# Spreading a routing decision over two turns, and a reordered lead-in, in an RWKV-then-router kernel

## The chip, the core and the metric

The kernel runs on one core of one Trainium2 chip. Its time is device microseconds from launch to end, the median of several runs. All arithmetic is float32. A core has five engines that run their own instruction queues: TensorE (PE, with its weight loads shown as PEld), VectorE (DVE), ScalarE (ACT), GpSimd (POOL) and SyncE (SP), which here only starts transfers. An engine executes its queue in program order; a semaphore makes it wait for another engine or a transfer.

## The reference, cut to what matters

A linear-attention recurrence over 768 steps (4 batches, 8 heads of 48) gives 3072 rows of 384. Each row is then sent to one of 8 experts, the one whose embedding is nearest in angle, and multiplied by its softmax weight.

```python
for t in range(S):                                   # S = 768
    cur = einsum('bhd,bhe->bhde', u[None] * kt, vt)
    y[:, :, t] = einsum('bhd,bhde->bhe', rt, state + cur)
    state = w[None, :, :, None] * state + einsum('bhd,bhe->bhde', kt, vt)
# x = y as rows (B*S, H*D) = (3072, 384)
logits = xn @ en.T / tau                             # xn, en: rows of norm one
expert_idx = argmax(logits, axis=1)                  # gate_w: its softmax weight
for e in range(E):                                   # E = 8, F = 1024
    h = maximum(x[mask] @ w1[e], 0.0)                # mask = expert_idx == e
    out[mask] = gate_w[mask, None] * (h @ w2[e])
```

## The kernel before

The sequence is cut into chunks of 128 steps; six chunks for each of four batches give 24 *units*. The decay `w` is clamped, its powers 1 to 128 are put into `wpow`, and two tables follow: `rpow` (powers over the middle power) scales the turned queries, and `kpow` (the reversed ones, turned) scales the keys. A *turn* of the loop `attention` has a unit in each stage: it turns the next unit's queries and keys (`rt`, `kt`), adds up its state (`st`), sums two products for the output (`y`), computes the next scores (`at`), and turns the output back to rows (`yrows`, then `X`). Between these lie the steps of the routing, a group of four units at a time: logits (`lgT`, `lg`), the choice, ranks, and lists of tokens for each expert (`take`, summed in `sums`).

After 16 of the 24 units are routed, the kernel *settles* which two experts are least loaded, so that the loading of their weights and one full tile of rows of each can start before the routing is over. Afterwards come those two early tiles, and then one `Block` per expert.

The start, cut:

```python
def build_first(k):
    ...                                              # wc is loaded by two DMAs
    ps = k.ps.tile([128, 512], F32, name="wake", tag="tp")
    for _ in range(WAKE):                            # WAKE = 3: products that warm TensorE up
        nc.tensor.matmul(ps, k.ones, wide, start=True, stop=True)
    ...                                              # 11 small memsets of Kpad and Rpad on GpSimd
    load(k, 0, nc.scalar)                            # K, R, V of unit 0; R on ScalarE's queue
    load(k, 1)
    load_consts(k)                                   # u_bc, emb, tau, wrow, all on ScalarE's queue
    build_consts(k)                                  # GpSimd: umask, states = 0, ent, iotas, ...
    for i in range(2, AHEAD - 1):
        load(k, i)
    own(k, 0)                                        # GpSimd: KU = K * u_bc * R

    nc.vector.tensor_scalar(wc, wc, W_MIN, W_MAX, ALU.max, ALU.min)
    t = pool.tile([128, NP, C], F32, name="wpow")
    ...                                              # 4 scans: powers; mid = 1 / t[:, :, 64]
    nc.vector.tensor_mul(kp, t[:, :, ::-1], over_i)
    ...                                              # TensorE turns kp into ps (kpT)
    nc.vector.tensor_mul(k.rpow, t, over_i)
    nc.vector.tensor_mul(k.Kpad[0]..., k.loaded[0][0]..., cols)   # cols = kpT
    turn_r(k, 0)                                     # rt, then RT = rt * rpow on VectorE
    k.kpow = pool.tile([128, H, D], F32, name="kpow")
    nc.vector.tensor_copy(k.kpow..., cols)
    turn_k(k, 0)                                     # kt, then KT = kt, copied by ScalarE
```

The state of a batch, whose first unit meets zeros:

```python
def carry(k, i):
    ...
    nc.vector.tensor_add(T[0:PP], T[0:PP], st[0:PP])
    nc.gpsimd.tensor_mul(T[0:PP], T[0:PP], k.wC[0:PP])
```

The loop, cut to what the change touches; `j = i - 12`, so `j == 8` is unit 20:

```python
    for i in range(-1, units):
        ...                                          # load, summed, turn_r, turn_k, scaled, own, states
        whole(choose, i - 3)
        ...
        on(own_sum, i + 1)                           # diag = sums of KU, VectorE
        if j == 7:
            load_, count = loads(k, "xp")
        if i == units - 2:
            own_rows_once(k, i + 1)                  # xd of the last unit, GpSimd
        if j == 9:
            perm = turner(k, k.by)                   # VectorE: hit, perm
            k.lists = turned_lists(k, perm, "st")    # TensorE: lists = sums x perm
            lists = taken_by_rank(k, k.lists)        # VectorE: none, take, gates
            first = [Early(k, r, *lists, w) for r, w in zip(LAST, k.weights)]   # gathers, GpSimd
            load_w2(k, number, k.weights[0][1])
        on(sums, i)                                  # y
        ...
        on(scores, i + 1)                            # at
        on(masked, i + 1, 0)
        on(rows, i)                                  # yrows, X
        on(masked, i + 1, 1)
        ...
        if j == 8:
            settle(k, load_, count)
            number = expert_number(k, LAST[0])
            load_w1(k, number, k.weights[0][0])

def settle(k, load, count):
    by = order(k, load)                              # VectorE: more, by
    nc.vector.tensor_scalar(k.settled, by, float(min(LAST)) - 1, None, ALU.max)
    expert_of(k, by)                                 # VectorE: eq, is_e, who
    k.by = by
    ...                                              # VectorE: lack, last, lack, cum
```

The last columns of an expert whose count isn't a multiple of 128 (two row tiles, three transposes each):

```python
    def rest(self):
        ...                                          # yT[:, m, :] for m = 0..2: TensorE, then a ScalarE copy
        for t, (_, _, gate, here) in list(enumerate(self.tiles))[2:]:
            ps = k.ps.tile(...)
            if n % 128:
                for m in range(NK):
                    nc.tensor.transpose(ps[0:here, m * 128 : (m + 1) * 128], yT[:, m, at], k.ident)
            ...
            nc.scalar.mul(y[0:here], ps[0:here, 0:DM], gate[0:here])
            self.put(t, y)
```

Of the kernel before, what the change touches and what calls it, by code (L numbers as in the profile page):

```python
# [47 lines left out]
def build_first(k):  # L48


    nc, pool = k.nc, k.aconst
    wc = pool.tile([128, NP], F32, name="wc")
    nc.vector.memset(wc, 1.0)
    with nc.allow_non_contiguous_dma(reason="384 words"):
        for s, q in ((0, nc.sync), (1, nc.scalar)):
            q.dma_start(out=wc[s * DP : s * DP + D, :], in_=k.w.rearrange("(p s) d -> s d p", s=2)[s])
    k.ones = k.const.tile([128, 128], F32, name="ones")
    nc.vector.memset(k.ones, 1.0)
    wide = k.work.tile([128, 512], F32, name="wide", tag="AT1")
    nc.vector.memset(wide, 1.0)  # L60
    k.ident = k.const.tile([128, 128], F32, name="ident")
    make_identity(nc, k.ident)

    ps = k.ps.tile([128, 512], F32, name="wake", tag="tp")
    for _ in range(WAKE):
        nc.tensor.matmul(ps, k.ones, wide, start=True, stop=True)
    for lst, name, count in ((k.Kpad, "Kpad", 4), (k.Rpad, "Rpad", AHEAD + 2)):
        for i in range(count):
            t = pool.tile([128, H, DP], F32, name=f"{name}{i}")
            nc.gpsimd.memset(t[:, :, D:DP], 0.0)  # L70
            lst.append(t)
    load(k, 0, nc.scalar)
    load(k, 1)
    load_consts(k)
    build_consts(k)
    for i in range(2, AHEAD - 1):
        load(k, i)
    own(k, 0)


    nc.vector.tensor_scalar(wc, wc, W_MIN, W_MAX, ALU.max, ALU.min)
    t = pool.tile([128, NP, C], F32, name="wpow")
    for p in range(NP):
        nc.vector.tensor_tensor_scan(
            t[:, p, :], wc[:, p : p + 1].to_broadcast([128, C]), k.ones, 1.0, ALU.mult, ALU.mult
        )
    mid = pool.tile([128, NP], F32, name="mid")
    nc.vector.reciprocal(mid, t[:, :, C // 2])
    over_i = mid[:, :, None].to_broadcast([128, NP, C])
    kp = k.work.tile([128, NP, C], F32, name="kp", tag="AT0")  # L90
    nc.vector.tensor_mul(kp, t[:, :, ::-1], over_i)
    ps = k.ps.tile([128, NP, 2, DP], F32, name="kpT", tag="xp")
    for p in range(NP):
        nc.tensor.transpose(ps[:, p].rearrange("q s d -> q (s d)"), kp[:, p, :], k.ident)
    k.rpow = pool.tile([128, NP, C], F32, name="rpow")
    nc.vector.tensor_mul(k.rpow, t, over_i)
    cols = ps[:, :, :, 0:D]
    nc.vector.tensor_mul(
        k.Kpad[0].rearrange("q (p s) d -> q p s d", s=2)[:, :, :, 0:D],
        k.loaded[0][0].rearrange("q (p s) d -> q p s d", s=2), cols,  # L100
    )
    turn_r(k, 0)
    k.kpow = pool.tile([128, H, D], F32, name="kpow")
    nc.vector.tensor_copy(k.kpow.rearrange("q (p s) d -> q p s d", s=2), cols)  # L104
    turn_k(k, 0)
    k.wC = t[:, :, C - 1 : C].to_broadcast([128, NP, D])


# [5 lines left out]
    return f  # L114


def load_consts(k):
    nc = k.nc
    k.u_bc = k.aconst.tile([128, H, D], F32, name="u_bc")
    nc.scalar.dma_start(  # L120
        out=k.u_bc.rearrange("p h d -> p (h d)"),
        in_=bass.AP(tensor=k.u.tensor, offset=k.u.offset, ap=[[0, 128], [1, DM]]),
    )
    k.emb_rows = k.aconst.tile([E, DM], F32, name="emb")
    nc.scalar.dma_start(out=k.emb_rows, in_=k.emb)
    k.tau_rows = k.aconst.tile([E, 1], F32, name="tau")
    nc.scalar.dma_start(
        out=k.tau_rows, in_=bass.AP(tensor=k.tau.tensor, offset=k.tau.offset, ap=[[0, E], [1, 1]])
    )
    k.wrow = k.aconst.tile([1, DM], F32, name="wrow")  # L130
    nc.scalar.dma_start(out=k.wrow, in_=k.w.rearrange("(o h) d -> o (h d)", o=1))


def build_consts(k):
    nc, pool = k.nc, k.const

    k.umask = pool.tile([128, 128], F32, name="umask")
    nc.gpsimd.memset(k.umask, 0.0)
    nc.gpsimd.affine_select(
        out=k.umask, in_=k.umask, compare_op=ALU.is_ge, fill=1.0,  # L140
        base=0, pattern=[[-1, 128]], channel_multiplier=1,
    )
    k.yT = [k.aconst.tile([128, 2, NP // 2, C], F32, name=f"yT{i}") for i in range(2)]
    for b in range(B):
        t = k.aconst.tile([128, NP, D], F32, name=f"state{b}")
        nc.gpsimd.memset(t, 0.0)
        k.state.append(t)
    k.ent = pool.tile([128, NK, 32], F32, name="ent")
    nc.gpsimd.memset(k.ent, 0.0)
    k.half = pool.tile([128, B], F32, name="half")  # L150
    nc.gpsimd.memset(k.half, 0.5)

    k.token = numbers(k, "token", [128, NCH, B], [[B * C, NCH], [C, B]], 1, 1)
    k.ebase = numbers(k, "ebase", [1, E], [[N, E]], 0, 0)
    k.rev = numbers(k, "rev", [128, E], [[-1, E]], E, 0)
    k.slots = numbers(k, "slots", [128, E, TM], [[TT, E], [1, TM]], 0, 0)
    k.lanes = numbers(k, "lanes", [128, 128], [[1, 128]], 0, 0)
    k.number = numbers(k, "number", [128, E], [[1, E]], 0, 0)
    k.qt = numbers(k, "qt", [2 * QS, QS], [[TM, 2], [0, E], [1, TM]], 0, 0)
    k.turned = numbers(k, "turned", [2 * QS, QS], [[0, 2], [1, E], [0, TM]], 1, 0)  # L160
    k.part = pool.tile([2 * QS, 1], I32, name="part")
    nc.gpsimd.iota(k.part, pattern=[[0, 1]], base=0, channel_multiplier=1)
    k.ring, k.turns = [pool.tile([128, DM], F32, name=f"G{i}") for i in range(8)], 0
    k.caps = pool.tile([1, E], F32, name="caps")
    for i, cap in enumerate(CAPS):
        nc.gpsimd.memset(k.caps[:, i : i + 1], float(cap))


    k.pos = pool.tile([128, NCH, B], I32, name="pos")
    k.gate = pool.tile([128, NCH, B], F32, name="gate")  # L170
    k.sums = pool.tile([2 * QS, 128], F32, name="sums")
    nc.gpsimd.memset(k.sums, 0.0)

    k.cum = pool.tile([128, E], F32, name="cum")

    k.fresh = pool.tile([128, E, B + 1], F32, name="fresh")
    nc.gpsimd.memset(k.fresh, 1.0)
    nc.gpsimd.memset(k.fresh[:, :, 0:1], 0.0)
# [203 lines left out]
def carry(k, i):  # L382
# [2 lines left out]
    T, st = k.state[i % B], k.st.pop(i, None)  # L385
    if st is None:
        return
    nc.vector.tensor_add(T[0:PP], T[0:PP], st[0:PP])
    nc.gpsimd.tensor_mul(T[0:PP], T[0:PP], k.wC[0:PP])


# [331 lines left out]
    return by  # L723


def settle(k, load, count):


    nc, pool = k.nc, k.const
    by = order(k, load)  # L730
    k.settled = pool.tile([128, E], F32, name="settled")
    nc.vector.tensor_scalar(k.settled, by, float(min(LAST)) - 1, None, ALU.max)
    expert_of(k, by)
    k.by = by
    lack = pool.tile([1, E], F32, name="lack")
    nc.vector.tensor_scalar(lack, count, -1.0, 128.0, ALU.mult, ALU.add)
    last = pool.tile([1, E], F32, name="last")
# [76 lines left out]
def attention(k):  # L814
# [17 lines left out]
    for i in range(-1, units):  # L832
# [19 lines left out]
        if 0 < i < units - 1:  # L852
            on(own_rows, i, 1)
        whole(norms, i - 2)
        whole(choose, i - 3)
        whole(before, i - 3)
        whole(located, i - 4)
        whole(gates, i - 5)
        whole(lanes, i - 5)
        whole(listed, i - 5)  # L860
        on(own_sum, i + 1)
        if 1 <= i < 4:
            next(emb)
        if j == 7:
            load_, count = loads(k, "xp")
        if i == units - 2:
            own_rows_once(k, i + 1)
        if j == 9:
            perm = turner(k, k.by)
            k.lists = turned_lists(k, perm, "st")  # L870
            lists = taken_by_rank(k, k.lists)
            first = [Early(k, r, *lists, w) for r, w in zip(LAST, k.weights)]
            load_w2(k, number, k.weights[0][1])
        on(sums, i)
        whole(exps, i - 4)
        on(carry, i)
# [1 line left out]
        on(masked, i + 1, 0)  # L878
        on(rows, i)
        on(masked, i + 1, 1)  # L880
        of_group(put, i)
        of_group(turn_rows, i - 1)
        whole(logits, i - 2)
        whole(ranks, i - 3)
        whole(taken, i - 5)
        if i == B:
            decays(k)
        if i == B + 1:
# [1 line left out]
        if 3 <= i < 3 + len(k.ring):  # L890
            k.nc.gpsimd.memset(k.ring[i - 3], 0.0)
        if j == 8:
            settle(k, load_, count)
            number = expert_number(k, LAST[0])
            load_w1(k, number, k.weights[0][0])
        if j == 10:
            to = outs(k, lists[0], E * TM)

# [196 lines left out]
class Block:  # L1095
# [167 lines left out]
    def rest(self):  # L1263
# [3 lines left out]
        if n % 128:  # L1267

            yT = k.hp.tile([128, NK, 256], F32, name="yT", tag="yT", bufs=1)
            for m in range(NK):  # L1270
# [4 lines left out]
                        start=(f == 0), stop=(f == NF - 1),  # L1275
                    )
                nc.scalar.copy(yT[:, m, 0:n], ps[:, 0:n])
        for t, (_, _, gate, here) in list(enumerate(self.tiles))[2:]:
            ps = k.ps.tile([128, TM * 128], F32, name="ps", tag="ps")
            if n % 128:  # L1280
                at = slice((t - 2) * 128, (t - 2) * 128 + here)
                for m in range(NK):
                    nc.tensor.transpose(ps[0:here, m * 128 : (m + 1) * 128], yT[:, m, at], k.ident)
            else:
                for f in range(NF):
                    mm(ps[:, 0:DM], h[:, f, t * 128 : (t + 1) * 128], w2[:, f, :], start=(f == 0), stop=(f == NF - 1))  # L1286
            y = k.gp.tile([128, DM], F32, name="y", tag="y", bufs=4)
# [261 lines left out]
```

## Time and profile before

| | |
|---|---|
| time, median of 3 runs | 419.84 us (419.61 to 421.07) |
| profiled execution | span 418.9 us, mean granted TensorE clock 0.978 |
| busy: PE, DVE, ACT, POOL | 397.3, 254.4, 172.3, 161.2 us |
| first scores start | 10.03 us |
| unit 20's `yrows` to unit 22's | 126.14 to 143.01 us |
| early tiles and experts | from 147.00 us on; to 400 us, no break of PE over 0.25 us |

The page cuts the span into 40 slices and gives the busy share of each engine and the TensorE clock that was granted. The timeline gives instructions in order of start, in microseconds: start, duration, engine, line of the kernel, operation, output <- inputs, shape, count; square brackets hold the idle time of that engine before, and what ended it. A float32 product is shown as two records, a transpose as one. Durations of neighbouring products overlap; the distance between starts says how long one takes in the stream.

### The profile page before, as it was taken

What the parts mean: (1) busy time and instruction counts of PE and PEld (TensorE: products, weight loads), DVE (VectorE), ACT (ScalarE), POOL (GpSimd) and SP (SyncE); (2) the same over time, 40 slices, a digit from 0 to 9 for tenths busy, and PEclk for the clock granted to TensorE, in tenths of its full rate; (3) what the DMA queues carried; (4) which work ended last, traced back from release to release, by engine and by line L of the source; (5) the groups of instructions that cost most, each with busy time, mean ns of one, the idle gap of its engine ahead of it and who ended that gap; (6) DMA issues with size and microseconds to landing.
All of it is one profiled execution on the core that took longest, in us unless ns stands there. A gap on an engine that the chain in (4) does not pass through costs nothing.

```text
span 418.9 us, 9283 instructions
## 1 busy us (share of the span) xinstructions
PE 397.3 (95%) x3542; PEld 355.0 (85%) x3542; DVE 254.4 (61%) x607; ACT 172.3 (41%) x517; POOL 161.2 (38%) x218
## 2 busy tenths in 40 slices
PE   6999999999996999999999999999999999999980
PEld 3888788888885887799999999999999999799580
DVE  7577986867775774176765767166376365565310
ACT  3677776767774521323333233223323233223020
POOL 8887687767666024230320602130340240300210
PEclk9899999999997999999999999999999999999996
DMA  9997576676714674034724704244164160240101
GB/s 163 182 230 165 116 151 130 147 146 144 156 45 154 244 271 139 26 95 184 243 83 152 238 14 161 79 172 153 46 221 151 43 222 2 51 157 1 56 21 42
DMA packets 93800, 54.39 MB, mean 130 GB/s; under 512 B 76937, under 2 KB 88380, under 8 KB 93746
## 3 DMA queue, kind: packets, MB, share of 16 engines
q1 hardware_dynamic: 89024, 43.85, 39.8%
q0 software_dynamic: 3296, 9.44, 6.9%
q8 instruction: 30, 0.49, 0.5%
q10 hardware_dynamic: 1426, 0.41, 0.5%
q14 instruction: 24, 0.20, 0.2%
HBM read 44.45 MB, written 9.63 MB: 129 GB/s over the span
## 4 chain that ended last, share of the span: by engine, by line
PE 82%; DVE 5%; POOL 4%; issue 3%; DMA 1%; ACT 1%; POOLq 0%; SPq 0%; DVEq 0%; ACTq 0%
PE ps L1169 24%; PE ps L1233 16%; PE ps L1273 5%; PE at L355 5%; PE y L416 5%; PE ps L1286 4%; PE early_y L988 3%; PE ps L1147 2%; PE early_h L979 2%; PE kt L343 2%; PE ps L1117 2%; PE y L407 2%; PE yrows L434 2%; PE st L376 2%; PE rt L332 2%
## 5 line engine op out<-in xcount | busy, mean ns | idle before, releaser
L1033 POOL DMA_INDIRECT out_dram<-y,to x25 | 30.0, 1198 | 174.6 <-issue 118.8
L1169 PE MATMUL ps<-xTe,w 128*128 128x192 f32 (+3 forms) x336 | 63.0, 327 | 0.0
L1169 PEld LDWEIGHTS ps<-xTe,w 128*128 128x128 f32 x336 | 55.9, 190 | 0.5
L361 DVE TENSOR_TENSOR AT<-at,umask 128x512 f32<-128x512 f32 x48 | 32.9, 686 | 27.4 <-PE at L355 27.4
L318 ACT ACTIVATE xd<-V,diag 128x48 f32<-128x48 f32 x184 | 46.2, 326 | 0.2 <-DVE diag L309 0.2
L1176 ACT ACTIVATE hT<-hT 128x384 f32<-128x384 f32 (+3 forms) x42 | 22.0, 523 | 32.4 <-DVE hT L1199 19.7
L1233 PE MATMUL ps<-Tw,Sh 128*128 128x192 f32 x192 | 32.5, 326 | 0.0
L1233 PEld LDWEIGHTS ps<-Tw,Sh 128*128 128x128 f32 x192 | 31.4, 190 | 0.0
L1024 POOL DMA_INDIRECT G<-xs,take x25 | 26.7, 1067 | 10.5 <-issue 4.3
L1169 PE MATMUL ps<-Tx,Sw 128*128 128x192 f32 (+3 forms) x168 | 29.7, 326 | 0.0
L355 PE MATMUL at<-RT,KT 48*128 48x128 f32 x384 | 28.8, 291 | 0.7 <-ACT KT L345 0.7
L355 PEld LDWEIGHTS at<-RT,KT 48*128 48x128 f32 x384 | 24.1, 193 | 5.3 <-issue 2.0
L1186 DVE TENSOR_TENSOR u<-ps,p 128x384 f32<-128x384 f32 (+3 forms) x14 | 7.8, 558 | 33.8 <-PE ps L1169 30.4
L1169 PEld LDWEIGHTS ps<-Tx,Sw 128*128 128x128 f32 x168 | 27.6, 190 | 0.1
L416 PE MATMUL y<-AT,V 128*48 128x128 f32 (+1 forms) x384 | 27.6, 287 | 0.0
L303 POOL TENSOR_TENSOR KU<-KU,Rpad 128x384 f32<-128x384 f32 x24 | 24.4, 1017 | 1.9
L522 ACT COPY xT<-xp 128x384 f32<-128x384 f32 x24 | 11.5, 479 | 31.7 <-PE xp L520 31.7
L416 PEld LDWEIGHTS y<-AT,V 128*48 128x48 f32 (+1 forms) x384 | 21.3, 129 | 3.6 <-issue 3.6
L302 POOL TENSOR_TENSOR KU<-K,u_bc 128x384 f32<-128x384 f32 x24 | 24.1, 1003 | 0.2 <-DMA u_bc<-in_u_dram 0.2
L1233 PE MATMUL ps<-w,hT 128*128 128x192 f32 x128 | 23.4, 326 | 0.0
L294 POOL TENSOR_TENSOR Kpad<-K,kpow 128x384 f32<-128x384 f32 x23 | 23.0, 1001 | 0.8 <-DVE kpow L104 0.8
L1196 ACT ACTIVATE hT<-ps 128x384 f32<-128x384 f32 (+3 forms) x14 | 6.9, 491 | 36.0 <-PE ps L1169 36.0
(239 smaller groups left out, 820.4 us busy)
## 6 DMA issues: line engine op xcount, KB each, us to landing
w<-in_moe_w_dram SPq DMA_DIRECT2D x16, 1536.0 KB, 7.0
K<-in_k_dram SPq DMA_DIRECT2D x24, 192.0 KB, 4.3
V<-in_v_dram SPq DMA_DIRECT2D x24, 192.0 KB, 4.1
xs<-X SPq DMA_DIRECT2D x24, 192.0 KB, 2.0
Rpad<-in_r_dram SPq DMA_DIRECT2D x23, 192.0 KB, 4.2
G<-xs,take POOLq DMA_INDIRECT x27, 3.3
out_dram<-y,to POOLq DMA_INDIRECT x25, 3.9
Rpad<-in_r_dram ACTq DMA_DIRECT2D x1, 192.0 KB, 4.1
```

The source lines that it names most:

```text
L294: k.nc.gpsimd.tensor_mul(k.Kpad[i % len(k.Kpad)][:, :, 0:D], k.loaded[i][0], k.kpow)
L302: nc.gpsimd.tensor_mul(KU, K, k.u_bc)
L303: nc.gpsimd.tensor_mul(KU, KU, R[:, :, 0:D])
L318: k.nc.scalar.mul(k.xd[i][:, h, :], V[:, h, :], diag[:, h : h + 1])
L355: nc.tensor.matmul(at[s][:, p, :], KT[rows, p, :], RT[rows, p, :], start=True, stop=True)
L361: k.nc.vector.tensor_mul(a, k.at[i][s], k.umask[:, None, :].to_broadcast([128, NP, C]))
L416: mm(y[s][u * DP : u * DP + n, q, :], V[:, h * D : h * D + n], AT[s][:, p, :], start=(c == 0 and q == 0), stop=True, skip_group_check=True,)
L1024: nc.gpsimd.indirect_dma_start(out=G[0:n, :], out_offset=None, in_=k.xs[:, :], in_offset=IndirectOffsetOnAxis(ap=take[0:n], axis=0), bound ...
L1033: put = k.nc.gpsimd.indirect_dma_start(out=k.out[:, :], out_offset=IndirectOffsetOnAxis(ap=to, axis=0), in_=y, in_offset=None, bounds_chec ...
L1169: nc.tensor.matmul(ps[:, j, :], weights[:, (f + j) * 128 : (f + j + 1) * 128], moving, start=(first and j == 0), stop=True, skip_group_che ...
L1176: nc.scalar.activation(h, h, ACT.Relu)
L1233: nc.tensor.matmul(ps, a[:, f, :], b[:, f, :], start=(first and f == 0), stop=(f == NF // 2 - 1), skip_group_check=True)
```

## The change

It has four parts.

1. *Settling.* Its steps go to four places in two turns (`j == 8` and `j == 9`, and the start of `j == 10`): the order of the experts at the end of turn 8, the number of the first expert and the load of its first weights in turn 9 after `own_sum`, the rest at the end of turn 9, and the product `lists`, the gathers and the load of the second weights in turn 10. `own_sum` and `own_rows_once` of the last unit move behind its masked scores, out of the way.
2. *Lead-in.* The clamp of `wc` moves from VectorE to GpSimd, `rpow` from one VectorE operation to four of ScalarE; the states aren't zeroed, the first unit of a batch copies instead; other constants are built after the first turn; `emb`, `tau` and `wrow` are loaded by SyncE after unit 3 instead of by ScalarE's queue; loads of units 1 to 3 come before them.
3. *Short idle products.* Two products whose results nobody reads (192 and 384 columns) lie between the transposes of the first unit; the warming products use another bank of PSUM.
4. *Last columns.* The six transposes of `rest` go `m` by `m` over both tiles, not tile by tile.

```diff
+    def busy(columns):
+        ps = k.ps.tile([128, 512], F32, name="wake", tag="y")
+        nc.tensor.matmul(ps[:, 0:columns], k.ones, wide[:, 0:columns], start=True, stop=True)
     for _ in range(WAKE):
-        nc.tensor.matmul(ps, k.ones, wide, start=True, stop=True)
+        busy(512)
 ...
-    load(k, 1)
-    load_consts(k)
-    build_consts(k)
-    for i in range(2, AHEAD - 1):
+    (u_bc is loaded here, on ScalarE's queue)
+    for i in range(1, AHEAD - 1):
         load(k, i)
+    load_rows(k)                                     # emb, tau, wrow, on SyncE's queue
+    nc.gpsimd.tensor_scalar(wc, wc, W_MIN, W_MAX, ALU.max, ALU.min)
+    build_numbers(k)                                 # umask, iotas and their casts
     own(k, 0)
-    nc.vector.tensor_scalar(wc, wc, W_MIN, W_MAX, ALU.max, ALU.min)
 ...
-    nc.vector.tensor_mul(k.rpow, t, over_i)
+    for p in range(NP):
+        nc.scalar.mul(k.rpow[:, p, :], t[:, p, :], mid[:, p : p + 1])
 ...
     turn_r(k, 0)
+    busy(192)
 ...
     turn_k(k, 0)
+    busy(384)
 ...
-    nc.vector.tensor_add(T[0:PP], T[0:PP], st[0:PP])
+    if i < B:
+        nc.vector.tensor_copy(T[0:PP], st[0:PP])
+    else:
+        nc.vector.tensor_add(T[0:PP], T[0:PP], st[0:PP])
 ...
+        if j == 10:
+            k.lists = turned_lists(k, perm, "st")
+            lists = taken_by_rank(k, k.lists)
+            first = [Early(k, r, *lists, w) for r, w in zip(LAST, k.weights)]
+            load_w2(k, number, k.weights[0][1])
         whole(choose, i - 3)
 ...
-        on(own_sum, i + 1)
+        if i < units - 2:
+            on(own_sum, i + 1)
 ...
         if j == 9:
-            perm = turner(k, k.by)
-            (lists, taken_by_rank, first, load_w2)
+            expert_of(k, by)
+            number = expert_number(k, LAST[0])
+            load_w1(k, number, k.weights[0][0])
         on(sums, i)
 ...
         on(masked, i + 1, 1)
+        if i == units - 2:
+            own_sum(k, i + 1)
+            own_rows_once(k, i + 1)
 ...
+        if i == 0:
+            build_constants(k)                       # half, ent, caps, sums, fresh
 ...
         if j == 8:
-            settle(k, load_, count)
-            number = expert_number(k, LAST[0])
-            load_w1(k, number, k.weights[0][0])
+            by = order(k, load_)
+        if j == 9:
+            settle(k, by, count)                     # settled, lack, last, lack, cum
+            perm = turner(k, by)
 ...
-        for t, (_, _, gate, here) in list(enumerate(self.tiles))[2:]:
-            ps = k.ps.tile(...)
-            if n % 128:
-                for m in range(NK):
-                    nc.tensor.transpose(...)
+        banks = [k.ps.tile(...) for _ in tiles]
+        for m in range(NK) if n % 128 else ():
+            for (t, (_, _, _, here)), ps in zip(tiles, banks):
+                nc.tensor.transpose(...)
```

## The prediction

> **What bounds the kernel now.** I read the page first: busy shares, slices, the chain.
>
> ```profile
> PE 397.3 (95%) x3542; PEld 355.0 (85%) x3542; DVE 254.4 (61%) x607; ACT 172.3 (41%) x517; POOL 161.2 (38%) x218
> ...
> PEclk9899999999997999999999999999999999999996
> ...
> PE 82%; DVE 5%; POOL 4%; issue 3%; DMA 1%; ACT 1%; POOLq 0%; SPq 0%; DVEq 0%; ACTq 0%
> ```
>
> TensorE is busy for 95% of the span and is 82% of the chain. So the end moves only if TensorE does less, waits less or runs at a better clock. Its clock dips in two slices of about 10.5 us, the second (10 to 21 us) and the thirteenth (126 to 136 us). There I went to the timeline of TensorE. First the lead-in:
>
> ```profile
> 6.90 0.63 PE L94 MATMUL kpT<-ident,kp 128*128 128x128 f32 x4 [1.05 <-DVE kp L91]
> 7.37 0.60 PE L332 MATMUL rt<-ident,Rpad 128*128 128x128 f32 x4
> 8.70 0.66 PE L343 MATMUL kt<-ident,Kpad 128*128 128x128 f32 x4 [0.73 <-DVE Kpad L98]
> 10.03 1.16 PE L355 MATMUL at<-RT,KT 48*128 48x128 f32 x16 [0.68 <-ACT KT L345]
> 11.12 1.01 PE L332 MATMUL rt<-ident,Rpad 128*128 128x128 f32 x4
> 11.93 1.06 PE L343 MATMUL kt<-ident,Kpad 128*128 128x128 f32 x4
> ```
>
> Three waits (1.05, 0.73, 0.68 us) precede the first scores. Then the same four transposes that took 0.60 and 0.66 us take 1.01 and 1.06. The stretches view gives a granted clock of 0.54, 0.50 and 0.68 between 11.12 and 15.2 us. Second, turn 9, where the settling lies:
>
> ```profile
> 128.08 0.60 PE L343 MATMUL kt<-ident,Kpad 128*128 128x128 f32 x4
> 132.00 0.66 PE L772 MATMUL lists<-perm,sums 128*128 128x64 f32 x2 [3.32 <-DVE perm L766]
> 132.59 1.12 PE L407 MATMUL y<-RT,state 48*64 48x128 f32 x16
> 133.64 1.95 PE L416 MATMUL y<-AT,V 128*48 128x128 f32 x16
> 135.52 2.08 PE L355 MATMUL at<-RT,KT 48*128 48x128 f32 x16
> ```
>
> An idle 3.32 us until VectorE has `perm`, then half speed up to 137.5 us. Between 26 and 128.7 us TensorE shows one wait of 0.20 us, and from 149 to 400 us it is busy for 250.3 of 251 us. So the middle turns and the experts are bound by TensorE itself, and a time saved ahead of them should reach the end.
>
> Why the lead-in is late, I read on VectorE:
>
> ```profile
> 3.31 1.11 DVE L81 TENSOR_SCALAR wc<-wc 128x4 f32<-128x4 f32 x1 [1.74 <-DMA wc<-in_w_dram]
> ...
> 6.07 0.69 DVE L91 TENSOR_TENSOR kp<-wpow,mid 128x512 f32<-128x512 f32 x1
> 6.68 1.51 DVE L96 TENSOR_TENSOR rpow<-wpow,mid 128x512 f32<-128x512 f32 x1
> ...
> 128.41 0.68 DVE L732 TENSOR_SCALAR settled<-by 128x8 f32<-128x8 f32 x1
> ```
>
> A clamp of 4 columns takes 1.11 us and `settled`, of 8, 0.68, where others of that size (`lack`, `last`) take 0.15. `rpow` takes 1.51 us, `kp` of the same size 0.69. Each long one overlaps GpSimd work and ends when a GpSimd operation does: `settled` at 129.09, `KU` on GpSimd at 129.07.
>
> [...] The trace has 128x48 products by a column of scales at 326 ns, and eight of them in 1.92 us.
>
> **The change, part by part.**
>
> *Settling.* What VectorE does between unit 22's masks and `perm` stays, but TensorE no longer stands before it. In turn 9 the queue holds: `yrows`, `xp`, `take`, `rt`, `kt`, `y`, scores. Turn 8, which has no `take`, took 121.48 to 126.14 = 4.66 us; `take` is 0.59; so turn 9 should take 5.25, from 126.14 to 131.4. In turn 10 `lists` stands behind `lg`. That turn took 137.53 to 143.01 = 5.48 and gets `lists` at full clock, about 0.17. Together 10.90, against 16.87 before (126.14 to 143.01).
>
> Is `perm` there in time? The second mask ends 1.85 us after its turn's `yrows` begin (126.14 to 127.99), here at 133.25. GpSimd has nothing to do then, so `settled` should be 0.15 to 0.2. From `who`'s end to `cum`'s end were 0.52 us (129.70 to 130.22), from `hit` to the end of `perm` 0.44 (131.41 to 131.85). So `perm` ends at about 134.45, and `lists` could start 0.15 later (131.85 to 132.00 before): 134.6. TensorE ends `lg` 2.8 us after `yrows` (137.53 to 140.32), at 134.2. A new wait of about 0.4 remains[...]. Saving: 16.87 - 10.90 - 0.4 = **5.6 us**. The other way to count agrees: 3.32 idle, plus the half-clock excess (0.33 `lists`, 0.47, 0.87, 0.92), minus 0.4.
>
> *Lead-in.* The weights `wc` are there at 3.25. GpSimd is through its 11 memsets at 2.92, so the clamp starts at once; an operation of a few columns takes it 0.1 to 0.2. The scans then start at about 3.6, not 4.45. They, `mid` and `kp` need 2.31 us as before (4.45 to 6.76): `kp` is done at 5.9, `kpT` at 6.65. VectorE is free then, since `rpow` is elsewhere (before, `Kpad` waited from 7.55 to 8.11 for it): `Kpad` 6.75 to 7.3. ScalarE has finished its casts at about 5.95 and makes `rpow` in four steps of 0.32 (estimated from 128x48: 0.24 apart[...]): 7.3, just in time for `RT`. Then `kt` 7.45 to 8.1, the copy `KT` (0.59) to 8.7, and the scores at **8.75** where they were at 10.03. I take off 0.15, as GpSimd's `umask` now meets the scans: 1.15 us. If the clock holds, the stretch from the scores' end to the next scores (11.12 to 15.22, 4.10) should be as in a warm turn (22.09 to 24.78, 2.69), or a little more, as ScalarE has eight `xd` there: 1.2 us. Lead-in: **2.3 us**. The idle products cost nothing if warm: 192 columns are two records, 0.33 us, in the gap of about 0.4 ahead of `kt`; 384 columns 0.65 in the gap of 0.65 ahead of the scores.
>
> *Last columns.* Before, two transposes run, and TensorE then waits until ScalarE has copied the third part of `yT`, and has four left. In the new order four run ahead of that wait. Two transposes of 0.115 us in each of three blocks: **0.6 us**.
>
> *Off the path.* The state copy replaces an addition of 0.35 us. The constants put about 1 us on GpSimd in turn 0 (0.09 + 0.17 + 0.32 + 0.19 + 0.12 + 0.11). GpSimd then runs without idle to 19.3 us as before, but a turn needs only 3.5 us of it where TensorE needs about 5.
>
> Sum: 5.6 + 2.3 + 0.6 = 8.5. I take off 0.6 for the clock[...]: the profiled run (420.69 us) lies 0.85 above the median, so the median may have lost less than this trace shows. 419.84 - 7.9 = **411.9 us**.
>
> **Rivals.** *A new wait in place of the old one:* `perm` later than TensorE needs it[...]. For it: `settled` did just that. Against: GpSimd is idle there, 130.1 to 133.4 before. It would leave 412.5 to 413. *Loads bound the first turns:* the stretches view shows the transfer engines full up to 36 us, and turns that begin 2.3 us earlier find their data no earlier. For it: `emb`, `tau` and `wrow` now stand ahead of unit 4 in SyncE's queue. Against: unit 4's key (issued 12.56, 4.3 us to land) was used at 22.07, a margin of 5 us, and no wait of TensorE for a transfer is in the trace. If right, the lead-in gives nothing: 414. *Idle products in the way:* at half clock they are 0.65 and 1.3 us and delay `kt` and the scores by up to 1: 413. *The early tiles wait for data:* rows gathered about 2.5 us later, used 5 us earlier; before, they took 6.2 us to land and lay about 7 us ready. Some tenths at most, but the margin is thin.
>
> **Range and chances.** [...] one of the larger rivals gives 413 to 414. I take 409.9 to 414.2. A gain of 2% ends at 411.4, so just beside my value: faster by over 2% has 0.40, within 2% 0.57, slower 0.03, since nothing adds work to TensorE but 0.98 us of idle products.
>
> **What would show it.** Right: in the changed profile the first scores start at 8.6 to 9.1; no transpose of 1.0 us between 9 and 15; `lists` with a wait under 0.6 us and products after it at 0.65, 1.08, 1.16; the two turns from unit 20's `yrows` in 11.0 to 11.6 us; `settled` under 0.3 us. Wrong: a PEclk digit of 7 or 8 in slices 2 or 13; TensorE waiting for a load in the first 40 us, or for `early_x`'s rows; a wait of over 1 us ahead of `lists`.

## The result, and the profile after

The changed kernel takes 413.38 us (median of 4 executions, 412.63 to 413.96), where the kernel before took 419.73 beside it: a ratio of 0.9851, 95% interval 0.981 to 0.9892. The point predicted was 411.9, so 1.5 us of the gain are missing. Yet the two profiled executions lie 8.4 us apart (spans of 418.9 and 410.5), and every step seems to be in them. The question for the experiments was which of the two accounts is typical.

From the page after, the busy line, the clock line and the chain:

```profile
PE 394.3 (96%) x3546; PEld 351.9 (86%) x3546; DVE 251.8 (61%) x605; ACT 173.0 (42%) x521; POOL 161.3 (39%) x215
...
PEclk9999999999999999999999999999999999999995
...
PE 84%; POOL 4%; DVE 3%; issue 3%; DMA 2%; ACT 1%; POOLq 0%; SPq 0%; ACTq 0%
```

Both dips of the clock line are gone, and TensorE is still the bound. Its timeline in the lead-in:

```profile
1.64 4.58 PE L66 MATMUL wake<-wide,ones 128*128 128x512 f32 x6 [1.64 <-DVE wide L60]
6.09 0.63 PE L101 MATMUL kpT<-ident,kp 128*128 128x128 f32 x4
...
8.70 1.16 PE L362 MATMUL at<-RT,KT 48*128 48x128 f32 x16
9.79 0.66 PE L339 MATMUL rt<-ident,Rpad 128*128 128x128 f32 x4
10.28 0.60 PE L350 MATMUL kt<-ident,Kpad 128*128 128x128 f32 x4
```

The first scores start at 8.70 (10.03 before), and the transposes behind them take 0.66 and 0.60 us (1.01 and 1.06 before). Unit 0's `yrows` start at 13.39 instead of 16.32: 2.93 us. The first line, the warming products, I had not shown in the prediction; it will matter. The two turns of the settling:

```profile
123.21 0.60 PE L444 MATMUL yrows<-ident,yT 112*128 112x112 f32 x4
...
128.38 0.60 PE L444 MATMUL yrows<-ident,yT 112*128 112x112 f32 x4
...
131.35 0.41 PE L779 MATMUL lists<-perm,sums 128*128 128x64 f32 x2
131.69 0.65 PE L417 MATMUL y<-RT,state 48*64 48x128 f32 x16
...
133.28 1.16 PE L362 MATMUL at<-RT,KT 48*128 48x128 f32 x16
134.38 0.60 PE L444 MATMUL yrows<-ident,yT 112*128 112x112 f32 x4
```

From unit 20's `yrows` to unit 22's it is 11.17 us, before 16.87: 5.70 us. `lists` starts 0.15 us behind the end of `perm` (131.20) and 0.12 behind that of the product `lg` ahead of it (131.23), so hardly a wait is left, and everything behind it runs at full speed. On VectorE `settled` now takes 0.16 us:

```profile
130.16 0.16 DVE L741 TENSOR_SCALAR settled<-by 128x8 f32<-128x8 f32 x1
...
130.95 0.25 DVE L773 TENSOR_SCALAR perm<-turned,myrank 128x64 f32<-128x64 f32 x1
```

At the end of the loop some of it is lost again. Timeline of all engines:

```profile
136.84 0.86 POOL L330 TENSOR_TENSOR xd<-V,diag 128x384 f32<-128x384 f32 x1 [1.69 <-ACT sq L537]
137.05 0.70 DVE L1030 SCALAR_TENSOR_TENSOR to<-batch,to 128x32 int32<-128x32 int32 x1
138.80 0.55 DVE L450 TENSOR_TENSOR X<-yrows,xd 128x384 f32<-128x384 f32 x1
138.94 0.55 PE L983 MATMUL early_x<-ident,G 128*128 128x128 f32 x3 [0.40 <-DMA G<-xs,take]
...
143.09 0.66 PE L692 MATMUL take<-lane,what 128*64 128x128 f32 x8 [0.52 <-POOL what L673]
```

TensorE waits 0.40 us for rows that were gathered, and 0.52 for GpSimd's `what`; an operation of VectorE on the outgoing rows' numbers (`to`) takes 0.70 us beside GpSimd's `xd` and the last `X` follows it. Unit 23's `yrows` start 8.63 us earlier than before (145.99 to 137.36), but the first expert's first product only 7.81 (173.80 to 165.99): 0.82 us are given back. The last columns add 0.66 (the lead grows to 8.02, 8.24 and 8.47 us after the three blocks), and their wait is gone from the list of TensorE's waits. Gone with it are those for `perm` (3.3), `kp` (1.0), `Kpad` and `KT` (0.7 each); the whole list is now:

```profile
PE wake L66 <- DVE wide L60: 1.6, 1, 1.6
PE take L692 <- POOL what L673: 0.5, 1, 0.5
PE early_x L983 <- DMA G<-xs,take: 0.4, 1, 0.4
PE kt L350 <- DVE X L450: 0.4, 1, 0.4
PE yrows L444 <- ACT yT L431: 0.3, 1, 0.3
PE rank L599 <- DVE state L398: 0.2, 1, 0.2
```

(The columns are the total, how often, and the longest.) In these two executions: 2.93 + 5.70 - 0.82 + 0.66 = 8.47. The medians differ by 6.35.

### The profile page after: what moved, and what is told of

Read it like the earlier page. It is cut to its first block, busy times and chain, and to the rows that moved or that the text cites. A ratio compares the mean times of both kernels' runs of the same rounds, so it can differ in the third digit from the quotient of the medians.

```text
span 410.5 us, 9292 instructions
## 1 busy us (share of the span) xinstructions
PE 394.3 (96%) x3546; PEld 351.9 (86%) x3546; DVE 251.8 (61%) x605; ACT 173.0 (42%) x521; POOL 161.3 (39%) x215
## 4 chain that ended last, share of the span: by engine, by line
PE 84%; POOL 4%; DVE 3%; issue 3%; DMA 2%; ACT 1%; POOLq 0%; SPq 0%; ACTq 0%
PE ps L1184 25%; PE ps L1248 16%; PE ps L1288 5%; PE at L362 5%; PE y L426 4%; PE ps L1302 4%; PE early_y L1003 3%; PE ps L1162 3%; PE early_h L994 3%; PE kt L350 2%; PE ps L1132 2%; PE rt L339 2%; PE st L383 2%; PE y L417 2%; PE yrows L444 2%
## 5 line engine op out<-in xcount | busy, mean ns | idle before, releaser
L362 PE MATMUL at<-RT,KT 48*128 48x128 f32 x384 | 27.9, 285 | 0.0
L426 PE MATMUL y<-AT,V 128*48 128x128 f32 (+1 forms) x384 | 26.2, 277 | 0.0
L426 PEld LDWEIGHTS y<-AT,V 128*48 128x48 f32 (+1 forms) x384 | 20.1, 124 | 3.5 <-issue 3.4
```

Of the source, the lines that this page charges most:

```text
L362: nc.tensor.matmul(at[s][:, p, :], KT[rows, p, :], RT[rows, p, :], start=True, stop=True)
L426: mm(y[s][u * DP : u * DP + n, q, :], V[:, h * D : h * D + n], AT[s][:, p, :], start=(c == 0 and q == 0), stop=True, skip_group_check=True,)
```

## Experiments: the parts one by one

**The settling alone.** The kernel before, with this and the moved `own_sum` and `own_rows_once`:

```diff
+        if j == 10:
+            k.lists = turned_lists(k, perm, "st") ...    # gathers, load_w2
...
         if j == 9:
-            perm = turner(k, k.by) ...                   # lists, gathers, load_w2
+            expert_of(k, by); number = ...; load_w1(...)
...
         if j == 8:
-            settle(k, load_, count) ...
+            by = order(k, load_)
+        if j == 9:
+            settle(k, by, count)
+            perm = turner(k, by)
```

> The kernel before with the settling part alone (four places in two turns), the lead-in, the idle products and the last columns as before. If the parts add up: in the trace the two turns from unit 20's yrows take 11.2 us instead of 16.9 (-5.7), and about 0.8 of it is given back at the early tiles, so the span is 4.9 shorter than the profiled one of before; the medians differ by 4.0 to 4.9. If the settling pays only together with the shorter lead-in (a new wait, or another clock phase), the two turns take over 11.6 us and the medians differ by under 4.

Measured: 414.13 us (413.52 to 414.9) against 419.68 (415.45 to 421.11, 19 executions): 5.55 us, ratio 0.9874 (0.9847 to 0.9901). That is more than expected. The two turns took 124.27 to 135.43 = 11.16 us, so no new wait and no half speed comes in (`y` behind `lists` 0.65 us, `at` 1.16); the settling pays by itself.

**The lead-in alone.** The changed kernel with the attention loop, `settle` and the last columns of before:

```diff
+    busy(192)  ...  busy(384)
-    nc.vector.tensor_scalar(wc, ...)
+    nc.gpsimd.tensor_scalar(wc, ...)
-    nc.vector.tensor_mul(k.rpow, t, over_i)
+    for p in range(NP): nc.scalar.mul(k.rpow[:, p, :], ...)
```

> The kernel before with the new lead-in and the idle products alone. Chain theory: first scores at 8.7 instead of 10.03 (-1.3), full clock behind them, unit 0's yrows at 13.4 instead of 16.3 (-2.9), and all of that still there at unit 20's yrows (126.14 to 123.2). The settling's wait of 3.3 us stays, but its half clock may fall differently[...]: the medians differ by 1.5 to 3. If the loads of the first units bound the turns that begin earlier, the gain shrinks between units 0 and 10 and the medians differ by under 1.

Measured: 419.56 us (417.92 to 421.24, 14 executions), ratio 1.0009 (0.9984 to 1.0034). The first expectation failed: there is no gain that the runs resolve (the interval allows 0.7 us at most). The second had the right size but the wrong reason: unit 0's `yrows` started at 14.62 and not at 16.32, and unit 20's `yrows` followed 109.88 us later, as before (109.82), so that no load bounds the turns. Its first scores stood at 9.93, not at 8.7. Its settling, same code as before, ran at half speed for a shorter time (the scores `at`, 2.08 us before, took 1.35 here), and its execution, 418.83 us, was below the median:

```profile
130.39 0.41 PE L782 MATMUL lists<-perm,sums 128*128 128x64 f32 x2 [3.35 <-DVE perm L776]
...
133.65 1.35 PE L362 MATMUL at<-RT,KT 48*128 48x128 f32 x16
```

**The wait filled.** The kernel before, with three idle products in the wait for `perm`:

```diff
             perm = turner(k, k.by)
+            fill = k.ps.tile([128, 512], F32, name="fill", tag="y")
+            for _ in range(3):
+                k.nc.tensor.matmul(fill, k.ones, k.rpow..., start=True, stop=True)
             k.lists = turned_lists(k, perm, "st")
```

> The kernel before with three idle products of 512 columns put into the wait for perm in turn 9. The wait stays as long (lists still starts at about 132.0), but TensorE is busy in it. If the half speed behind it comes from the idle time, it goes: lists 0.33, y 0.65 and 1.08, scores 1.16, unit 22's yrows at about 140.4 instead of 143.0, so 2.6 us of the 5.7 are clock and 3.3 are the wait itself; medians 2.0 to 2.6 apart. If the half speed has another cause (power, the products themselves), nothing changes.

Measured: 416.09 us (415.58 to 416.97), 3.6 us less than before, ratio 0.9925 (0.9898 to 0.9952). `lists` still waits for `perm`, 0.76 us behind the idle products, but runs at full speed:

```profile
125.58 2.74 PE L872 MATMUL fill<-rpow,ones 128*128 128x512 f32 x6
129.08 0.41 PE L772 MATMUL lists<-perm,sums 128*128 128x64 f32 x2 [0.76 <-DVE perm L766]
129.41 0.65 PE L407 MATMUL y<-RT,state 48*64 48x128 f32 x16
```

So the half speed came from the idle time. In the traces the two turns take 14.38 us with the wait filled (123.20 to 137.58), against 16.87 in the first trace of before and 11.16 with the settling alone. By the medians the half speed was worth 3.6 of the settling's 5.55 us, more than the 2.6 read from the profiled execution; the waiting itself, net of what is given back at the early tiles, only 2.0.

**Without the idle products.** The changed kernel minus `busy(192)` and `busy(384)`.

> The changed kernel without its two idle products of 192 and 384 columns. If transposes and waits do not keep the clock, the clock falls to half behind the first scores as before: four transposes at 1.0 us instead of 0.6, unit 0's yrows at 14.4 to 15.0 instead of 13.39, and the time 1.0 to 1.6 longer. If the shorter waits alone keep the clock (the gaps are 0.4 and 0.65 us), nothing changes: within 0.2.

Measured: 413.74 us (412.91 to 414.13). No half speed follows, though TensorE waits:

```profile
8.01 0.66 PE L348 MATMUL kt<-ident,Kpad 128*128 128x128 f32 x4 [0.21 <-DVE Kpad L106]
9.34 1.16 PE L360 MATMUL at<-RT,KT 48*128 48x128 f32 x16 [0.67 <-ACT KT L350]
10.44 0.65 PE L337 MATMUL rt<-ident,Rpad 128*128 128x128 f32 x4
```

From `kpT` to the first scores it is 2.58 us here (6.76 to 9.34), 2.61 with the idle products (6.09 to 8.70). They cost nothing and kept nothing that these executions would have lost; that the lead-in needs products between its transposes to hold its clock was not shown. The 0.4 us between the medians isn't resolved: the ranges overlap.

## Experiments: the lead-in

**The lead-in of before, in the changed kernel.** Settling and last columns as after, the rest as before (the settling alone, plus the new order of the transposes).

> The changed kernel with the lead-in of before (clamp on VectorE, rpow on VectorE, states zeroed, no idle products); settling and last columns as after. It measures the lead-in against the changed kernel on the same chip. Prediction's theory (the chain of VectorE bounds the lead-in, 1.15 us, and the clock adds 1.2): 2.3 us slower than the changed kernel, about 415.7. New theory (TensorE's three warming products of 512 columns stand ahead of kpT; they last 4.2 to 5.5 us according to when the clock rises, so the chain is mostly hidden behind them; and with the settling's wait gone the other executions keep their clock): within 0.5 us, about 413.6. In its trace kpT then starts within 0.3 us of the end of the warming products, or, where these end before 6.0, the clamp decides.

**The changed kernel once more.** The same kernel, unedited.

> The changed kernel once more, a second trace and times on the same chip as the other three. If the lead-in depends on the clock's phase, its first scores lie elsewhere than 8.70 (up to 9.9) and the warming products last other than 4.58 us (up to 5.5); if not, 8.70 and 4.58 again within 0.1. Median 413.0 to 413.8.

**Warming products that start earlier:**

```diff
     for _ in range(WAKE):
-        busy(512)
+        ps = k.ps.tile([128, 512], F32, name="wake", tag="y")
+        for c in range(4):
+            nc.tensor.matmul(ps[:, c * 128 : (c + 1) * 128], k.ones, k.ones, ...)
```

> The changed kernel, whose warming products read 128 columns of ones (twelve of them) instead of 512 columns of the tile wide (three): the same columns, but they needn't wait for wide and start at 1.1 instead of 1.64. If the warming products bound the lead-in, they end 0.5 earlier, kpT starts at 6.1 to 6.5 instead of up to 6.9, and the median is 0.3 to 0.5 us lower than the changed kernel's. If VectorE's chain bounds it (kpT waits for kp), nothing changes.

**The kernel before, traced twice more**, unedited.

> A second trace of the kernel before. If the profiled execution of before was a typical one: first scores at 10.03, transposes of 1.0 us behind them, half speed of 6.8 us behind lists. If the lead-in depends on the clock's phase: warming products of 5.2 to 5.5 us, kpT right behind them at 6.7 to 6.9, first scores at 9.5 to 9.9 and no half speed behind them; unit 0's yrows at 14.0 to 14.5 instead of 16.32; half speed behind lists of 3.4 to 10.2 us.

> A third trace of the kernel before, for the same question: how often the half speed in the lead-in comes, and how long the one behind lists lasts. By the clock's phase: no transposes of 1.0 us between 9 and 15 us in at least one of the two traces; the half speed behind lists lasts a whole number of steps of about 3.4 us.

Measured: with the lead-in of before 413.81 us (413.41 to 414.32), the changed kernel 413.21 (412.72 to 413.31; ratio to before 0.9837, 0.9813 to 0.9861). The lead-in is worth **0.6 us**, and not 2.3; the two ranges don't overlap. The earlier warming products gave 413.29 (412.9 to 413.42): `kpT` started at 6.38 in their trace, as expected, but the expected gain of 0.3 to 0.5 us over 413.21 did not come.

Two more traces of before show why. First the second trace, VectorE and then TensorE:

```profile
3.19 1.23 DVE L81 TENSOR_SCALAR wc<-wc 128x4 f32<-128x4 f32 x1 [1.62 <-DMA wc<-in_w_dram]
...
6.07 0.69 DVE L91 TENSOR_TENSOR kp<-wpow,mid 128x512 f32<-128x512 f32 x1
...
6.68 0.68 DVE L96 TENSOR_TENSOR rpow<-wpow,mid 128x512 f32<-128x512 f32 x1
```

```profile
1.62 5.49 PE L66 MATMUL wake<-wide,ones 128*128 128x512 f32 x6 [1.62 <-DVE wide L60]
6.91 0.65 PE L94 MATMUL kpT<-ident,kp 128*128 128x128 f32 x4
...
9.54 1.16 PE L355 MATMUL at<-RT,KT 48*128 48x128 f32 x16 [0.68 <-ACT KT L345]
10.63 0.66 PE L332 MATMUL rt<-ident,Rpad 128*128 128x128 f32 x4
```

Then VectorE in the third, where the warming products last 5.32 us and `kpT` starts at 6.78:

```profile
3.17 0.29 DVE L81 TENSOR_SCALAR wc<-wc 128x4 f32<-128x4 f32 x1 [1.60 <-DMA wc<-in_w_dram]
...
5.11 0.69 DVE L91 TENSOR_TENSOR kp<-wpow,mid 128x512 f32<-128x512 f32 x1
```

The third has `kp` almost 1 us earlier, as its clamp took 0.29 us and not 1.23. It makes hardly any difference, because `kpT` stands in TensorE's queue behind the warming products. In all fourteen traces:

| trace | warming products end | `kp` ends | `kpT` starts | first scores |
|---|---|---|---|---|
| before, profiled first | 5.85 | 6.76 | 6.90 | 10.03 |
| before, second | 7.11 | 6.76 | 6.91 | 9.54 |
| before, third | 6.94 | 5.80 | 6.78 | 9.36 |
| wait filled (lead-in of before) | 6.27 | 5.79 | 6.11 | 8.69 |
| settling alone (lead-in of before) | 7.11 | 6.77 | 6.92 | 9.74 |
| lead-in of before, rest as after | 7.11 | 6.77 | 6.92 | 9.72 |
| after, profiled first | 6.22 | 5.94 | 6.09 | 8.70 |
| after, second | 6.82 | 5.92 | 6.65 | 9.23 |
| lead-in alone | 7.13 | 5.90 | 6.92 | 9.93 |
| after without idle products | 6.93 | 5.96 | 6.76 | 9.34 |
| after, warming products earlier | 6.59 | 5.91 | 6.38 | 9.06 |
| after, both moves (next section) | 5.95 | 5.90 | 6.05 | 8.66 |
| after, only the load later (next section) | 6.39 | 5.93 | 6.23 | 8.81 |
| after, only `to` later (next section) | 6.99 | 5.91 | 6.83 | 9.41 |

In eleven of the rows the warming products end at 6.27 or later, and `kpT` starts 0.16 to 0.21 ahead of their modelled end. In the other three (5.85, 6.22 and 5.95) it starts 0.14 or 0.15 behind the end of `kp`: there VectorE's chain sets the start, or both do, and one of these is the profiled execution of after, another that of before. On average the first scores start at 9.51 with the lead-in of before (six traces) and at 9.15 with the new one (the seven with the warming products unmoved), 0.36 us earlier. The end of the warming products is not set by the code alone: the same three products take 4.23 to 5.49 us. The filling products of the same shape took 2.74 at full speed, and 5.49 is twice that; so I read 5.49 as half speed throughout, and the shorter times as a clock that rose on the way. The loads of their weights agree: in the trace of the settling alone (5.49 us) they start 0.85 or 0.86 us apart up to the last, in the first trace of before (4.23 us) up to the one at 4.35, with the next 0.48 later. Where the clamp was short and the clock rose early, even the lead-in of before has its first scores at 8.69, within 0.03 us of the earliest of the changed kernel. In the earlier-started version they took the full 5.49 us (1.10 to 6.59): half a microsecond earlier, but with no shorter time from a rise of the clock. One trace doesn't tell how often that is so, and the median shows no gain: in the times this test leaves the explanation unconfirmed.

The other half of the chain, `rpow` on VectorE ahead of `Kpad`, was no steady cost either. It took 1.51 us in the first trace of before, beside GpSimd's `KU`, and 0.68 or 0.69 in the five other traces with the same code, where `KU` began later than it (6.76 us or after). In these five the stretch from the start of `kpT` to the first scores is 2.58 to 2.63 us where `kpT` ran at full speed, as with the new lead-in (2.58 to 2.61), against 3.13 in the first trace. So moving `rpow` to ScalarE gains nothing that these traces show outside the first one.

The half speed *behind* the first scores, 1.2 us of my sum, was in the first trace of before (11.3 to 14.7 us, granted clock 0.50) and in no other of the fourteen. The three kernels that have the lead-in of before without the long idle wait at `lists` (settling alone, wait filled, and the one here) ran 17 times in all, never at a mean clock under 0.988, where the trace with the dip had 0.978. The clamp of `wc` too differs from run to run: with the code of before it took 1.11, 1.23, 0.29, 0.20, 1.15 and 1.27 us in the first six rows of the table.

## Experiments: what is given back at the early tiles

A measure that leaves out where the clock was low: the time from unit 22's `yrows` to the start of the last group of products. It is 262.64 us in the first trace of before (143.01 to 405.65), 262.64 in the second, 262.65 in the third; without the 0.66 of the last columns, 261.98. The changed kernel needs 262.81 (134.38 to 397.19) and 262.94 (134.92 to 397.86): 0.8 and 1.0 us given back.

**Both moves:** the load of the first expert's second weights one turn later, and `to` behind the loop.

```diff
         if j == 10:
             first = [Early(k, r, *lists, w) for r, w in zip(LAST, k.weights)]
-            load_w2(k, number, k.weights[0][1])
...
-        if j == 10:
-            to = outs(k, lists[0], E * TM)
+        if j == 11:
+            load_w2(k, number, k.weights[0][1])
...                                                      # behind the loop and its last groups
+    to = outs(k, lists[0], E * TM)
```

> The changed kernel with the load of the first expert's second weights one turn later and the operation that makes the outgoing rows' numbers moved behind the loop. If the gathered rows are late because that load shares the transfer engines with them, the wait ahead of early_x (0.40 to 1.08 us in three traces) and the one for X go: 0.5 to 0.9 us faster than the changed kernel. If the gather's own latency, or the first load, sets it, the wait stays: within 0.2.

Measured: **411.98 us** (411.81 to 412.59), ratio to before 0.9815 (0.9791 to 0.984), 1.2 less than the changed kernel's 413.21 beside it. It is faster than both kernels; its slowest execution is faster than the fastest of the changed kernel beside it. The wait for the rows is gone, that for `what` shrinks to 0.23:

```profile
138.47 0.49 PE L990 MATMUL early_x<-ident,G 128*128 128x128 f32 x3
138.62 0.55 DVE L450 TENSOR_TENSOR X<-yrows,xd 128x384 f32<-128x384 f32 x1
...
142.54 0.66 PE L692 MATMUL take<-lane,what 128*64 128x128 f32 x8 [0.23 <-POOL what L673]
```

**One move each:** only the load later; only `to` later.

> The changed kernel with only the load of the first expert's second weights one turn later; the outgoing rows' numbers stay where they were. The version with both moves was 1.2 us faster than the changed kernel. If the load's share of the transfer engines is the cause, this one has 0.9 to 1.2 of it (412.0 to 412.4), and the wait ahead of early_x is gone while the operation to still takes 0.70. If the two moves work by different waits in one chain, 0.3 to 0.7 of it.

> The changed kernel with only the outgoing rows' numbers behind the loop; the load stays in turn 10. If the load is the cause, the rows are still late: the wait ahead of early_x stays at 0.4 to 1.1 and grows by what X comes earlier, and the time is within 0.3 of the changed kernel. If the 0.70 us operation ahead of X is a cause of its own, 0.3 to 0.7 faster.

Measured: the load alone 412.73 us (412.16 to 413.57), `to` alone 413.23 (412.68 to 413.6), neither taken beside the changed kernel's 413.21. Both ranges overlap its range, and the load alone misses the 412.0 to 412.4 expected of it if it were the whole cause. By the measure above, the given-back part is 0.47 with the load moved (134.60 to 397.05), 0.84 with `to` moved (135.08 to 397.90), 0.33 with both (134.33 to 396.64), and 0.83 and 0.96 with neither. So the load is the larger cause: moving it takes away 0.36 to 0.49 us of the 0.50 to 0.63 that both moves take, and `to` counts only once the rows are there; by itself it leaves waits of 0.55 and 0.32 for the rows. The gathers of these rows show the load's part (126 to 146 us; the last column is the median time to landing in us), first of the changed kernel, then with only the load moved:

```profile
G<-xs,take POOLq DMA_INDIRECT x2, 6.2
```

```profile
G<-xs,take POOLq DMA_INDIRECT x2, 4.1
```

With only `to` moved it is 6.3. That the two slow each other by sharing the transfer engines fits this, but was not separated from other ways.

What stays open: the traces show 0.50 to 0.63 us of gain for both moves, and the medians 1.2. The rest may be the lead-in, as the first scores of that one trace stood at 8.66; this wasn't separated.

## Why the prediction was right, and where it was wrong

**Settling, 5.6 us: right, but by numbers that partly offset.** The working held: turn 9 took 5.17 us (predicted 5.25), turn 10 6.00 (5.65 and a wait of 0.4), and alone it is worth 5.55. Of turn 10, `lists` took 0.34 us and not 0.17, and the wait ahead of it 0.1 to 0.2 and not 0.4; that one so short would leave the clock alone was my estimate, and no half speed followed it (`y` 0.65 us, `at` 1.16). But the 5.6 left out what the early tiles give back, and the trace that I read had lost less here than the two taken later: 5.70 less 0.8 is 4.9, and the agreement with 5.55 is in part luck. Around `lists` the half speed lasts 6.8 us in the first trace (130.7 to 137.6, with TensorE idle until 132.0), 10.2 in the second and the third, 3.4 in the kernel with the lead-in alone. In the second trace it reaches from `lists` to `kt`, and `yrows` and `rt`, 0.60 and 0.66 us at full speed, take 1.01 and 1.12:

```profile
133.46 2.08 PE L355 MATMUL at<-RT,KT 48*128 48x128 f32 x16
135.47 1.01 PE L434 MATMUL yrows<-ident,yT 112*128 112x112 f32 x4
...
138.48 1.12 PE L332 MATMUL rt<-ident,Rpad 128*128 128x128 f32 x4
```

There the two turns took 19.01 us, so that the change saves 7.85 of them, less about 1 at the early tiles. The times of before fall into steps by their mean clock: 18 of 39 executions at 0.976 or 0.977, 420.6 us on average; 11 at 0.980 or 0.981, 419.4; 6 at 0.985, 418.1; one at 0.988, 415.45; three lie between. The steps fit three, two, one and no stretches of 3.4 us at half speed, as one of them takes 0.004 off the mean over 419 us (half of 3.4, divided by 419); where in the execution they lie the mean doesn't tell. How soon the clock returns once TensorE is busy again can't be read from one trace: in the second the clock was at half from 129.9 to 140.1, and TensorE was busy from 129.94 on without a break, while in the kernel with the lead-in alone it was back 3.7 us after the start of `lists` (130.39 to 134.1). What sets these lengths was not shown.

**Lead-in, 2.3 us: wrong, the step that failed.** "The scans then start at about 3.6 ... `kpT` at 6.65 ... the scores at 8.75 where they were at 10.03": this followed VectorE's chain from `wc` to `kp` and let `kpT` follow it. The times came out (scans at 3.59, `kp` done at 5.94, and `rpow` in four ScalarE steps of 0.32 us, which had been my estimate). But TensorE's own queue has the warming products ahead of `kpT`, and in eight of the thirteen traces that start them alike they end at 6.8 to 7.1, later than `kp` does in either kernel. The 4.23 us of the first trace hid this, and its `rpow` of 1.51 us, of which the chain counted the delay to `Kpad`, was in no other trace. I looked for half speed behind the idle wait and behind the first scores, and not in the warming products at the start, which took 4.23 to 5.49 us. The second half, "if the clock holds ... 1.2 us", rested on a stretch of half speed that one trace of before had and none of the others. Measured in place of 2.3: 0.6. That the time still fell into the range is partly luck: its upper end came from the rivals, and the largest of them, the loads with 414, did not come true.

**The signs named.** In the first profile after, those for right came (8.70, no slow transposes, 11.17, 0.16), and so did one of those for wrong: TensorE waits 0.40 us for the rows of `early_x`. In the second trace of the changed kernel the first scores stood at 9.23, outside 8.6 to 9.1.

**Last columns, 0.6: right**, 0.66 in the traces; between the kernels with the settling alone and with the settling and the new order the medians differ by 0.3, within their ranges.

**Rivals.** *A new wait in place of the old one*: no, `perm` ended at 131.20 and `lists` followed at 131.35. *Loads bound the first turns*: no, unit 0's `yrows` to unit 20's are 109.82 us in both profiled executions. *Idle products in the way*: no, 0.03 us. *The early tiles wait for data*: right in kind. I gave it some tenths and didn't put it in the sum; it is 0.8 to 1.0, and the load that I had let move with the gathers accounts for 0.4 to 0.5 of it.

**The correction for the clock, 0.6 off**, had the right sign but was too small and named no place: what the profiled execution overstated was the lead-in. Put together from the experiments: 5.55 + 0.6 + 0.3 to 0.66 = 6.5 to 6.8, against 6.35 and 6.4 measured.

Of the slow operations of VectorE, `settled` took 0.68 us beside GpSimd's `KU` (128.07 to 129.07) and 0.16 in the trace after, with GpSimd idle from 127.1 to 132.5; that the two slow each other fits this, but was not separated from other causes. That each long operation ends with a GpSimd operation, as the prediction read it, doesn't hold for `rpow`: it ended at 8.19, the two `KU` at 7.63 and 9.03. For the clamp GpSimd's work beside it may be the cause too, but what decides stays open: the same code took 0.29 us when it began at 3.17, and 1.27 and 1.23 when it began at 3.16 and 3.19.

## What to carry to other kernels

Before a wait is counted as gain, look at what else stands ahead of the instruction in its own engine's queue, and take two or three traces: here the trace read first had waits in the lead-in that most others lacked, and a shorter half speed in the settling than the two later ones. Here an idle stretch of 3.3 us in TensorE cost more by the slow clock behind it (3.6 us) than by the waiting (2.0), so filling it with idle products already brought more than half of what removing it did (3.6 of 5.55). When a decision is moved earlier, move the gathers with it, but look at whether a large load that moves along delays them: here they took 6.2 us to land beside it and 4.1 without it.

## What the runs showed of the hardware that I had not expected

- The warming products at the start take 4.23 to 5.49 us for the same work, while the granted clock is given as 1.00 throughout: if 5.49, twice the 2.74 us of the same products later, is half speed, the column doesn't show it there.
- VectorE's clamp of `wc`, begun between 3.16 and 3.31, takes 0.2 to 0.3 or 1.1 to 1.3 us, and its start doesn't tell which. In the second case it ends at 4.42 to 4.44, whenever it began, 0.2 behind the last of GpSimd's four memsets of the states.
- Half speed lasted 3.4, 6.8 and twice 10.2 us around the end of the same wait, by the clock column whole multiples of 3.41 within its rounding, although TensorE was busy without a break from `lists` on.
